# Loads, stores and zero fill of a decode layer's backward pass: one DMA queue in a fixed order instead of two side by side

## The chip, the cores and the metric

The kernel runs on one core of a Trainium2 chip. A core has a matrix engine (TensorE, PE in the profile), three engines for vectors and elements (VectorE, DVE; ScalarE, ACT; GpSimd, POOL) and SyncE (SP), which here only issues DMAs. Data move between the device memory and the on-chip memory through 16 DMA engines. A DMA is issued by an engine's instruction stream, in order: an instruction that waits for a semaphore holds up all that stand behind it in the same stream. The metric is the device time of one execution in microseconds; lower is better.

## The reference

A layer with pre-normalised sliding-window attention over a cache and a gated feed-forward part, for one decoded token in each of two batch rows, and the gradients of its eight inputs:

```python
def _A_ref(x, k_cache, v_cache, wq, wo):          # Hq 32, Hkv 8, Dh 128, Sk 32768, W 4096
    q = (x @ wq) ...
    k = jnp.repeat(k_cache[:, :, Sk - W:, :], rep, axis=1)
    v = jnp.repeat(v_cache[:, :, Sk - W:, :], rep, axis=1)
    p = _softmax(einsum("bhqd,bhkd->bhqk", q, k) * Dh ** -0.5)
    return einsum("bhqk,bhkd->bhqd", p, v) ... @ wo

def _B_ref(x, w_gate, w_up, w_down):
    return (_gelu(x @ w_gate) * (x @ w_up)) @ w_down

h = x + _A_ref(_layernorm(x), k_cache, v_cache, wq, wo)
h2 = h + _B_ref(_layernorm(h), w_gate, w_up, w_down)
# outputs: h2 and, for the given grad_out, d x, d k_cache, d v_cache, d wq, d wo, d w_gate, d w_up, d w_down
```

Only the last 4096 of 32768 cache rows take part. So the gradients of both caches (2 x 8 x 32768 x 128 in bf16 each) are zero in the other 28672 rows of every one of the 16 (batch row, group) pairs. Those zeros have to be written: 32 regions of 7 MiB, 224 MiB together.

## The kernel before, in words

**Stages.** Batch row b is handled as `attention(b)`, `middle(b)` and `score_grads(b)`, first for b = 0 and then for b = 1; after that come the weight gradients and the cache gradients.

- `attention(b)` runs over eight groups g, each with its 4096 keys K(b,g) and values V(b,g), 1 MiB each. For a group, PE transposes the keys (`kt_unit`, L378, in four units), multiplies them with the queries (`s_unit`, L388), a softmax follows (`softmax`, L392 to L415), and then eight units of products of keys and probabilities (`m_unit`): four element-wise products on DVE into one of the small `pK` buffers (L422) and the matmuls into `oPK_ps` (L429) and `M_ps` (L433). In the code the transposes and softmax of group g + 1 are woven into the units of group g. `finish` copies the group's sums out (L438 to L441).
- `middle(b)` does the output projection, the feed-forward part forwards and backwards, and the way back through `wo`. Its first matmul (L522) needs the row of x, which is loaded again for b = 1 (`load_rows`, L135).
- `score_grads(b)` transposes the values (L656) and forms the gradient of the scores. For b = 1 the weight gradients `wo`, `w_down`, `w_gate`, `w_up` are made piece by piece between its units (`grad_units`, L727) and stored when a group of pieces is whole (L737, L755, L762).
- Then follow `wq` (L807, stores at L810) and the cache gradients: 16 stores of 2 MiB (L836 for the matmuls, L844 for the stores) out of eight staging buffers.

**Memory.** Keys, values and weights share one block of on-chip memory with fixed offsets. K(0,g) has four slots of its own, so that K(0,g+4) can be loaded only after group g is finished. V(b,g) has one slot for each g; V(1,g) can be loaded only after score_grads(0) has transposed V(0,g). K(1,0), K(1,1) go to the `w_down` slot, K(1,2) to K(1,4) into the value slots 5 to 7, K(1,5) into the slot of K(1,0), K(1,6) into that of K(1,1), and K(1,7) into that of K(1,5). V(1,5) to V(1,7) follow into the slots of K(1,2) to K(1,4).

**Order.** SyncE and GpSimd issue in the order of the program text (`manual_schedule`, L676). The order of PE, DVE and ACT is made by a planner, which uses estimated costs and arrival times of the loads; it is fixed when the kernel is built. `prefetch(b, g)` (L306) is called at the start of each group and stands for the place in the text at which loads are issued. All loads but two rows go on SyncE's queue, and so do the stores of the weight gradients. GpSimd makes the zero tile `zt` (one row of 2048 bytes per partition; the DMA widens it to 32-bit zeros) after `wq` has landed (L315). It then issues 29 of the 32 regions (`zero_cast`), with nothing in between. The last three regions are cut in pieces of 1, 1, 1, 2, 2 MiB (`ZERO_CUTS`) and follow the 16 stores of the cache gradients, one piece after each but the last (`zero_next`).

In three regions a part of the zeros is written with 15 or 12 rows instead of 128 (`ZERO_PARTS`), so that not all of the DMA engines get an equal share there. In the built kernel each DMA of GpSimd waits for the completion of the one eight before it.

Of the kernel before, what the change touches and what calls it, by code (L numbers as in the profile page):

```python
# [8 lines left out]
F32 = mybir.dt.float32  # L9
U8 = mybir.dt.uint8  # L10
U32 = mybir.dt.uint32
ACT = mybir.ActivationFunctionType
ALU = mybir.AluOpType
# [3 lines left out]
P = 128  # L17
# [7 lines left out]
F = 1792  # L25
# [43 lines left out]
def kernel(ctx, tc, A_x, A_k_cache, A_v_cache, A_wq, A_wo, B_x, B_w_gate, B_w_up, B_w_down, grad_out,  # L69
# [36 lines left out]

    ZERO_PARTS = {8: ((4, 1), (15, 2), (2, 2), (15, 14), (12, 2), (P, 4), (16, 7)), 16: ((4, 1), (15, 2), (2, 2), (15, 14), (12, 2), (P, 4), (16, 7)), 24: ((3, 16), (15, 2), (3, 4), (15, 18), (12, 2), (P, 4))}
    ZERO_FIRST, ZERO_CUTS = 29, (1, 1, 1, 2, 2)

    def zero_cast(i):  # L110
        dst, done = zero_regions[i].bitcast(F32), 0
        for rows, n in ZERO_PARTS.get(i, ((P, ZPK // P),)):
            src = zt[0:rows * (P // rows):P // rows, :]
            nc.gpsimd.dma_start(out=dst[done * ZE:(done + rows * n) * ZE].rearrange("(p k e) -> p k e", p=rows, k=n),  # L114
                                in_=src.unsqueeze(1).to_broadcast([rows, n, ZE]))
            done += rows * n
        assert done == ZPK

    zero_pieces = []
    for i in range(ZERO_FIRST, len(zero_regions)):  # L120
        done = 0
        for k in ZERO_CUTS:
            zero_pieces.append(zero_regions[i].bitcast(F32)[done:done + P * k * ZE].rearrange("(p k e) -> p k e", p=P, k=k))
            done += P * k * ZE
        assert done == ZPK * ZE

    def zero_next():
        if zero_pieces:
            dst = zero_pieces.pop(0)
            nc.gpsimd.dma_start(out=dst, in_=zt[:].unsqueeze(1).to_broadcast([P, dst.shape[1], ZE]))  # L130

# [16 lines left out]

    def load_k(b, g):
        Kt[b, g] = at(K_OFF[b][g], [P, NJ, DH], BF16, f"K{b}_{g}")  # L150
        nc.sync.dma_start(out=Kt[b, g][:], in_=Kv[:, b, g, :, :])

    def load_v(b, g):
        Vt[b, g] = at(OFF_V + g * 8 * KIB, [P, NJ, DH], BF16, f"V{b}_{g}")
        nc.sync.dma_start(out=Vt[b, g][:], in_=Vv[:, b, g, :, :])

# [10 lines left out]
    def load_wg():  # L167
        nc.sync.dma_start(out=wg[:], in_=B_w_gate.rearrange("(p r) f -> p r f", r=NDR))

    def load_wu():  # L170
        nc.sync.dma_start(out=wu[:], in_=B_w_up.rearrange("(p r) f -> p r f", r=NDR))

# [133 lines left out]
    def prefetch(b, g):  # L306
        if b == 0:
            if g == 0:
                load_k(0, 0)
                load_wd(OFF_WD0)  # L310
                load_v(0, 0)
                for i in range(1, 4):
                    load_k(0, i)
                    load_v(0, i)
                nc.gpsimd.tensor_scalar(out=zt[:], in0=wq_sb[:, 0, 0:ZE // 2].bitcast(U8),  # L315
                                        scalar1=0, scalar2=None, op0=ALU.mult)
                for i in range(ZERO_FIRST):
                    zero_cast(i)
            elif g + 3 < HKV:
                load_k(0, g + 3)  # L320
                load_v(0, g + 3)
            elif g == 5:
                nc.sync.dma_start(out=wo_sb[:], in_=A_wo.rearrange("(p r) n -> p r n", r=NOR))
            elif g == 6:
                load_wg()
            elif g == HKV:
                load_wu()
                load_k(1, 0)
                load_k(1, 1)
        else:  # L330
            if g == 0:
                for i in range(5):
                    load_v(1, i)
                for i in range(2, 5):
                    load_k(1, i)
            elif g == 1:
                load_k(1, 5)
            elif g == 2:
                load_k(1, 6)
            elif g < 6:  # L340
                load_v(1, g + 2)
            elif g == 6:
                load_k(1, 7)
            elif g == HKV:
                load_rows(nc.sync)
                load_wd(OFF_WD)
# [351 lines left out]
    with tc.tile_pool(name="ps_G", bufs=2, space=PSUM) as ps_G:  # L698
# [35 lines left out]

        for (r0, nr) in ((0, 14), (14, 14), (28, 4)):
            add_group([D] * nr, lambda k, r0=r0: Ro_flat[:, (r0 + k)::NOR], lambda k: DH_bf[:],
                      lambda st, r0=r0, nr=nr: nc.sync.dma_start(out=gwo_v[:, r0:r0 + nr, :],  # L737
                                                                 in_=st[:, :nr * D].rearrange("p (a n) -> p a n", n=D)))
        row_box = {}

        def rows_from_T(key, srcT_bf):
# [3 lines left out]
            for r in range(NFR):  # L745
                if r == 8:
# [7 lines left out]
        add_group([D] * NFR, lambda k: row_box["act"][:, k::NFR], lambda k: dh2_bf,  # L754
                  lambda st: nc.sync.dma_start(out=gwd_v, in_=st[:, :NFR * D].rearrange("p (a n) -> p a n", n=D)))  # L755
        for (key, srcT, o_dram) in (("dg", dgT_bf, out_6), ("du", duT_bf, out_7)):
            grad_units.append(lambda key=key, srcT=srcT: rows_from_T(key, srcT))
            o_v = o_dram.rearrange("(p r) f -> p r f", r=NDR)
            pieces = [(r, f0, fl) for r in range(NDR) for (f0, fl) in ((0, 512), (512, 512), (1024, 512), (1536, 256))]
            add_group([fl for (_, _, fl) in pieces], lambda k, pieces=pieces: ln2_bf[:, pieces[k][0]::NDR],  # L760
                      lambda k, key=key, pieces=pieces: row_box[key][:, pieces[k][1]:pieces[k][1] + pieces[k][2]],
                      lambda st, o_v=o_v: nc.sync.dma_start(out=o_v, in_=st[:, :NDR * F].rearrange("p (r f) -> p r f", r=NDR)))  # L762
        g_next = [0]
# [9 lines left out]
    with tc.tile_pool(name="ps_W2", bufs=2, space=PSUM) as ps_W, \  # L773
# [27 lines left out]
        for r in range(NDR):  # L801
            st = at(OFF_WQ + r * 8 * KIB, [P, HQ * DH], BF16, "gq")
            for c4 in range(4):
                ps = ps_G.tile([P, 1024], F32, tag="ps_g", name="ps_gq")
                for q in range(2):
                    col0 = c4 * 1024 + q * 512
                    nc.tensor.matmul(out=ps[:, q * 512:(q + 1) * 512], lhsT=L_bf[:, r::NDR],  # L807
                                     rhs=Ro_flat[:, col0:col0 + 512], start=True, stop=True)
                evac(st[:, c4 * 1024:(c4 + 1) * 1024], ps[:])
            nc.sync.dma_start(out=gwq_v[:, r, :], in_=st[:])  # L810

    with tc.tile_pool(name="ps_G3", bufs=3, space=PSUM) as ps_G, \
# [4 lines left out]
        def bd_of(n):  # L817
# [3 lines left out]
            return build_bd(OFF_BD + n * 8 * KIB, rowsb[:], f"bd{n}")  # L821
        nxt = bd_of(0)
        for n, (b, what) in enumerate(jobs):
            rhs_bd = nxt
            lhs_bf, dst_v = (ds_bf[b], dKv) if what else (p_bf[b], dVv)
            for gq in range(2):
# [15 lines left out]
                for a in range(2):  # L842
                    g0 = gq * 4 + a * 2
                    nc.gpsimd.dma_start(out=dst_v[:, b, g0:g0 + 2, :, :], in_=sts[a][:])  # L844
                    zero_next()
                if gq == 0 and n + 1 < len(jobs):
# [28 lines left out]
```

## Time and profile before

| What | Value |
| --- | --- |
| Median of 3 runs | 791.56 us (791.41 to 791.93) |
| Profiled execution, own time | 791.69 us |
| Its span, first to last instruction | 790.0 us |
| Mean granted TensorE clock | 0.807 |
| PE, DVE, ACT, POOL busy | 72%, 60%, 36%, 8% |
| Bytes moved by DMA | 332.44 MB, mean 421 GB/s |
| HBM read, written | 49.30 MB, 282.33 MB |
| attention(0), last matmul of `M_ps` | ends at about 135 us |
| attention(1), matmuls of `M_ps` | about 250 to 387 us |
| First store of a weight gradient issued (L737) | 484.2 us |
| First store of a cache gradient issued (L844) | 619.8 us |

The page cuts the span into 40 equal slices of 19.75 us. Its DMA row gives the mean busy share of the 16 DMA engines in tenths, its GB/s row what they moved. The queue rows give packets, megabytes, and the time that the packets took as a share of 16 engines' span: q0 is GpSimd's queue, q1 SyncE's; packets of two queues overlap in time, so that the shares may sum to more than one. In the rows of waits the numbers are the time in total, how often, and the longest. In a timeline each row has the start, the duration, the engine and the line, and in brackets how long the engine had been idle before and what ended that.

### The profile page before, as it was taken

Reading aid. Unit: us, or ns where it says so; the run is one execution under the profiler, and the core shown is the slowest. Engines: PE = TensorE matmul, PEld = TensorE weight load, DVE = VectorE, ACT = ScalarE, POOL = GpSimd, SP = SyncE. Lnnn points to the kernel's source line nnn. Section 1 sums busy time; section 2 is a strip of 40 time slices with the busy share of each in tenths; the row PEclk is TensorE's granted clock in tenths of the full one; section 3 lists DMA queues with packets and bytes.
Section 4 is the critical chain, followed back from the end, with each engine's and each line's share of the span. In section 5 each row is a group of like instructions: output and inputs, shape, how many; then the busy total and the mean of one; then the engine's idle time right before and its main releaser. Section 6 shows DMA issues by size and latency. Waiting matters only on the chain. (4 is left out here: it accounts for less than half of the span.)

```text
span 790.0 us, 12468 instructions
## 1 busy us (share of the span) xinstructions
PE 564.9 (72%) x5096; PEld 301.0 (38%) x5096; DVE 472.6 (60%) x1161; ACT 280.9 (36%) x406; POOL 65.5 (8%) x97
## 2 busy tenths in 40 slices
PE   3899998795888899825558779797886775857000
PEld 3655554544665555313225544343332221212000
DVE  2699998238335899824612676755457998757000
ACT  1534330234344433102012426544443674646000
POOL 4300000000020000000020000000100111111100
PEclk9899999786799999877876869855685897779555
DMA  8999999999999999999999999999999999999997
GB/s 366 416 419 422 419 424 428 424 430 427 428 419 418 426 424 426 425 425 430 427 428 428 428 428 427 422 430 424 430 426 427 424 430 426 428 428 427 428 429 295
DMA packets 41418, 332.44 MB, mean 421 GB/s; under 512 B 2432, under 2 KB 2448, under 8 KB 2576
## 3 DMA queue, kind: packets, MB, share of 16 engines
q0 software_dynamic: 34416, 268.44, 88.6%
q1 hardware_dynamic: 6932, 63.19, 37.5%
q8 instruction: 40, 0.66, 0.3%
q10 hardware_dynamic: 12, 0.01, 0.2%
q14 instruction: 18, 0.15, 0.0%
HBM read 49.30 MB, written 282.33 MB: 420 GB/s over the span
## 5 line engine op out<-in xcount | busy, mean ns | idle before, releaser
L422 DVE TENSOR_TENSOR mem<-mem,ee 128x512 bf16<-128x512 bf16 x512 | 180.6, 414 | 34.0 <-PE M_ps L433 33.8
L433 PE MATMUL M_ps<-mem 128*128 128x512 bf16 x512 | 140.2, 392 | 5.3 <-DVE mem L422 4.8
L836 PE MATMUL ps_g<-mem 128*128 128x512 bf16 x256 | 85.6, 448 | 38.4 <-DVE mem L91 36.8
L91 DVE CAST mem<-ps_g 128x512 bf16<-128x512 f32 x128 | 82.9, 686 | 26.7 <-DMA out_dram<-mem 15.3
L93 ACT CAST mem<-ps_g 128x512 bf16<-128x512 f32 x128 | 74.3, 586 | 51.4 <-PE ps_g L836 49.5
L380 ACT COPY mem<-KT_ps 128x1024 bf16<-128x1024 bf16 x64 | 63.1, 1013 | 77.4 <-PE KT_ps L378 72.7
L114 POOL DMA_DIRECT2D out_dram<-zt x46 | 36.9, 976 | 503.6 <-DMA out_dram<-zt 503.2
L378 PE MATMUL KT_ps<-ident_bf,mem 128*128 128x128 bf16 x512 | 44.7, 229 | 28.3 <-DMA mem<-in_A_k_cache_dram 23.3
L836 PEld LDWEIGHTS <-mem 128*128 128x128 bf16 x256 | 28.1, 110 | 95.3 <-issue 84.7
L433 PEld LDWEIGHTS <-mem 128*128 128x128 bf16 x512 | 43.8, 99 | 48.8 <-issue 15.5
L254 PE MATMUL ps_tb<-ident_bf,mem 128*128 128x128 bf16 x480 | 55.9, 250 | 7.1 <-ACT mem L258 2.7
L93 ACT COPY mem<-ps_tb 128x512 bf16<-128x512 bf16 x44 | 25.8, 586 | 67.5 <-PE ps_tb L254 62.7
L254 PEld LDWEIGHTS <-mem 128*128 128x128 bf16 x480 | 37.4, 128 | 32.3 <-issue 31.0
L656 PE MATMUL VT_ps<-ident_bf,mem 128*128 128x128 bf16 x512 | 46.8, 239 | 2.6 <-ACT mem L93 1.1
L665 PE MATMUL dP_ps<-mem 128*128 128x512 bf16 x128 | 44.3, 435 | 4.5 <-ACT mem L93 4.5
L656 PEld LDWEIGHTS <-mem 128*128 128x128 bf16 x512 | 36.6, 107 | 27.9 <-issue 20.5
L378 PEld LDWEIGHTS <-mem 128*128 128x128 bf16 x512 | 33.7, 103 | 34.0 <-DMA mem<-in_A_k_cache_dram 23.9
L93 ACT COPY mem<-VT_ps 128x1024 bf16<-128x1024 bf16 x31 | 31.7, 1022 | 34.0 <-PE VT_ps L656 32.8
L91 DVE COPY mem<-ps_tb 128x512 bf16<-128x512 bf16 x44 | 18.7, 424 | 41.6 <-PE ps_tb L254 40.2
L727 PE MATMUL ps_gr<-mem 2*128 2x512 bf16 (+1 forms) x78 | 33.7, 498 | 11.7 <-DVE mem L747 7.4
L91 DVE CAST mem<-ps_gr 128x512 bf16<-128x512 f32 (+1 forms) x38 | 24.7, 654 | 27.9 <-PE ps_gr L727 27.9
L91 DVE COPY mem<-VT_ps 128x1024 bf16<-128x1024 bf16 x33 | 23.1, 700 | 28.0 <-PE VT_ps L656 27.5
(244 smaller groups left out, 619.7 us busy)
## 6 DMA issues: line engine op xcount, KB each, us to landing
out_dram<-zt POOLq DMA_DIRECT2D x26, 7168.0 KB, 102.4
out_dram<-mem POOLq DMA_DIRECT2D x16, 2048.0 KB, 34.0
mem<-in_A_k_cache_dram SPq DMA_DIRECT2D x16, 1024.0 KB, 20.7
mem<-in_A_v_cache_dram SPq DMA_DIRECT2D x16, 1024.0 KB, 21.4
out_dram<-zt POOLq DMA_DIRECT2D x3, 4096.0 KB, 58.5
out_dram<-zt POOLq DMA_DIRECT2D x6, 2048.0 KB, 33.0
out_dram<-zt POOLq DMA_DIRECT2D x9, 1024.0 KB, 34.6
out_dram<-mem SPq DMA_DIRECT2D x5, 1792.0 KB, 18.7
```

The lines of the kernel that those rows point to most:

```text
L91: nc.vector.tensor_copy(out=out, in_=in_)
L93: nc.scalar.copy(out=out, in_=in_)
L114: nc.gpsimd.dma_start(out=dst[done * ZE:(done + rows * n) * ZE].rearrange("(p k e) -> p k e", p=rows, k=n), in_=src.unsqueeze(1).to_broadc ...
L254: nc.tensor.transpose(out=ps[:, a, :], in_=src_block(a), identity=ident_bf[:])
L378: nc.tensor.transpose(out=KT_ps[:, jj, :], in_=Kt[b, g][:, u * 8 + jj, :], identity=ident_bf[:])
L380: nc.scalar.copy(out=KT[:], in_=KT_ps[:])
L422: nc.vector.tensor_tensor(out=pk[:, :, i, :].rearrange("p j (d t) -> p j d t", t=2), in0=Kb[:, j0:j0 + pk_j, :].rearrange("p j (d t) -> p ...
L433: nc.tensor.matmul(out=M_ps[:], lhsT=Vt[b, g][:, j, :], rhs=pk[:, jj, :, :].rearrange("p i d -> p (i d)"), start=(j == 0), stop=(j == NJ - 1))
L656: nc.tensor.transpose(out=VT_ps[:, jj, :], in_=Vt[b, g][:, a * 8 + jj, :], identity=ident_bf[:])
L665: nc.tensor.matmul(out=dP_ps[:, c, :], lhsT=dOpad[:, w0:w0 + P], rhs=VT[:, c * 4:(c + 1) * 4, :].rearrange("d a k -> d (a k)"), start=(i = ...
L727: nc.tensor.matmul(out=ps[:, :n], lhsT=lhsT_fn(k), rhs=rhs_fn(k), start=True, stop=True)
L836: nc.tensor.matmul(out=ps[:, a2, :], lhsT=lhs_bf[:, jp * P:(jp + 1) * P], rhs=rhs_bd[:, ap * 2 + a2, gq * 4:(gq + 1) * 4, :].rearrange("q ...
```

## The change

Key, value, `wo`, `w_gate` and `w_up` loads and the stores of the weight gradients move from SyncE's to GpSimd's queue. The zeros are counted in columns of 1 MiB (224 in all), and `zeros(n)` issues the next n of them. Each load or store on GpSimd's queue is followed by a fixed number of columns. What stays on SyncE: x, `wq`, K(0,0), V(0,0), K(0,1), V(0,1), `w_down` both times, K(1,7), the rows for the second half, and the gradient of x. The zero tile is now made from K(0,0) instead of `wq`, and the first zeros follow K(0,2) to V(0,3). The three regions with unequal parts are 5, 15 and 26 instead of 8, 16 and 24, with somewhat different parts.

```diff
-    ZERO_PARTS = {8: ((4, 1), (15, 2), (2, 2), (15, 14), (12, 2), (P, 4), (16, 7)), 16: (...same...), 24: ((3, 16), (15, 2), (3, 4), (15, 18), (12, 2), (P, 4))}
-    ZERO_FIRST, ZERO_CUTS = 29, (1, 1, 1, 2, 2)
+    ZERO_PARTS = {5: ((4, 1), (15, 2), (2, 2), (15, 18), (12, 1), (128, 4), (16, 4)), 15: (...same...), 26: ((3, 16), (15, 2), (3, 4), (15, 18), (12, 2), (128, 4))}
+    TAIL_ZEROS = (1, 1, 1, 2, 2, 1, 1, 1, 2, 2, 1, 1, 1, 2, 2, 0)
+    def zeros(n):
+        while n:
+            i, c = divmod(z_cols[0], ZCOLS)
+            parts = ZERO_PARTS[i] if c == 0 and n >= ZCOLS and i in ZERO_PARTS else ((P, min(n, ZCOLS - c)),)
+            done = c * P
+            for rows, k in parts:
+                zero_rows(zero_regions[i].bitcast(F32)[done * ZE:(done + rows * k) * ZE], rows, k)
+                done += rows * k
+            z_cols[0] += done // P - c
+            n -= done // P - c
...
-        nc.sync.dma_start(out=Kt[b, g][:], in_=Kv[:, b, g, :, :])
+        eng.dma_start(out=Kt[b, g][:], in_=Kv[:, b, g, :, :])       # eng=nc.gpsimd unless given; V alike
...
     def prefetch(b, g):
             if g == 0:
-                load_k(0, 0)
+                load_k(0, 0, nc.sync)
                 load_wd(OFF_WD0)
-                load_v(0, 0)
-                for i in range(1, 4):
+                for i in range(2):
+                    load_v(0, i, nc.sync)
+                    if i == 0:
+                        load_k(0, 1, nc.sync)
+                nc.gpsimd.tensor_scalar(out=zt[:], in0=Kt[0, 0]...)
+                for i in range(2, 4):
                     load_k(0, i)
                     load_v(0, i)
-                nc.gpsimd.tensor_scalar(out=zt[:], in0=wq_sb...)
-                for i in range(ZERO_FIRST):
-                    zero_cast(i)
+                zeros(5)
             elif g + 3 < HKV:
                 load_k(0, g + 3)
+                zeros(1)
                 load_v(0, g + 3)
+                zeros(2)
             elif g == 5:
-                nc.sync.dma_start(out=wo_sb[:], ...)
+                nc.gpsimd.dma_start(out=wo_sb[:], ...)
+                zeros(2)
             elif g == 6:
                 load_wg()
+                zeros(7)
             elif g == HKV:
                 load_wu()
                 load_k(1, 0)
                 load_k(1, 1)
+                zeros(29)
         else:
             if g == 0:
                 for i in range(5):
                     load_v(1, i)
+                    zeros(1)
                 for i in range(2, 5):
                     load_k(1, i)
+                    zeros(1 if i < 4 else 8)
             elif g == 1:
                 load_k(1, 5)
+                zeros(5)
             elif g == 2:
                 load_k(1, 6)
+                zeros(5)
             elif g < 6:
                 load_v(1, g + 2)
+                zeros((5, 6, 60)[g - 3])
             elif g == 6:
-                load_k(1, 7)
+                load_k(1, 7, nc.sync)
...
+        def store(out, in_, n):
+            nc.gpsimd.dma_start(out=out, in_=in_)
+            zeros(n)
-        for (r0, nr) in ((0, 14), (14, 14), (28, 4)):        # wo gradient, stores on nc.sync
+        for (r0, nr, nz) in ((0, 14, 3), (14, 14, 1), (28, 4, 9)):   # stores by store(..., nz)
...                                                          # w_down: store(..., 8); w_gate 5; w_up 13
-            nc.sync.dma_start(out=gwq_v[:, r, :], in_=st[:])
+            nc.gpsimd.dma_start(out=gwq_v[:, r, :], in_=st[:])
+            zeros(1 if r < NDR - 1 else 10)
...
                     nc.gpsimd.dma_start(out=dst_v[:, b, g0:g0 + 2, :, :], in_=sts[a][:])
-                    zero_next()
+                    zeros(tail_zeros.pop(0))
```

## The prediction

> **What bounds the kernel now.** First the 40 slices of the page, then its DMA queues and the chain of waits:
>
> ```profile
> DMA  8999999999999999999999999999999999999997
> GB/s 366 416 419 422 419 424 428 424 430 427 428 419 418 426 424 426 425 425 430 427 428 428 428 428 427 422 430 424 430 426 427 424 430 426 428 428 427 428 429 295
> q0 software_dynamic: 34416, 268.44, 88.6%
> q1 hardware_dynamic: 6932, 63.19, 37.5%
> ```
>
> The DMA engines are busy from the second slice to the last. 332.4 MB must move, 268.4 of them on GpSimd's queue (q0), 63.2 on SyncE's (q1). No compute engine is near its limit (PE 72%, DVE 60%), so the kernel ends when the bytes are through: the chain's largest item is the stores at the end (14% of the span). A change can help only by a higher rate and hurt only by time in which no transfer is queued. The rate is not the same everywhere. Windows (us, engines, then clock, DMA share, GB/s):
>
> ```profile
> 20.00:60.00 40.00, 37.55 (x529) 24.68 (x527) 32.14 (x101) 17.98 (x23) 7.56 (x9) 0.91 1.13 417
> 160.00:200.00 40.00, 30.24 (x276) 19.64 (x275) 23.63 (x62) 16.29 (x30) 1.29 (x2) 0.76 1.15 429
> 210.00:250.00 40.00, 32.72 (x423) 22.87 (x422) 13.99 (x29) 20.97 (x22) 5.77 (x6) 1.00 1.14 421
> 420.00:480.00 60.00, 46.85 (x382) 27.07 (x381) 37.56 (x97) 23.41 (x41) 1.71 (x3) 0.77 1.15 427
> ```
>
> Where only zeros move (160:200, 420:480) it is 427 to 429; where SyncE's loads mix in (20:60, 210:250), 417 to 421. Then what GpSimd waits for:
>
> ```profile
> POOL out_dram L114 <- DMA out_dram<-zt: 503.2, 30, 37.2
> 19.35 7.61 POOL L114 DMA_DIRECT2D out_dram<-zt  x8 [0.31 <-POOL zt L315]
> 59.10 0.60 POOL L114 DMA_DIRECT2D out_dram<-zt  x1 [32.14 <-DMA out_dram<-zt]
> 619.82 0.73 POOL L844 DMA_DIRECT2D out_dram<-mem  x1 [60.29 <-DVE mem L91]
> ```
>
> Eight DMAs go out, and each further one waits for the one eight before it. A zero region is 7 MiB, so up to 56 MiB lie ahead: GpSimd's 60.3 us wait before the first cache-gradient store leaves the DMA engines busy all the same. SyncE's DMAs are those that wait on compute:
>
> ```profile
> 206.42 17.68 SPq L155 DMA_DIRECT2D mem<-in_A_v_cache_dram  x5
> 291.63 30.78 SPq L155 DMA_DIRECT2D mem<-in_A_v_cache_dram  x3
> 335.20 0.33 SPq L151 DMA_DIRECT2D mem<-in_A_k_cache_dram  x1
> 484.19 14.30 SPq L737 DMA_DIRECT2D out_dram<-mem  x3
> ```
>
> These are a V load for each slot that score_grads(0) frees, three V loads paced by groups 2 to 4 of the second attention, K(1,7) after group 5, and the wo gradient. Today a late one costs no DMA time, because zeros fill in. Last, how long K(1,7) takes to arrive (PE in time):
>
> ```profile
> 339.73 0.81 PE L433 MATMUL M_ps<-mem 128*128 128x512 bf16 x3
> 363.26 1.89 PE L378 MATMUL KT_ps<-ident_bf,mem 128*128 128x128 bf16 x16 [22.72 <-DMA mem<-in_A_k_cache_dram]
> ```
>
> Issued at 335.20, used at 363.26: 28 us behind the zeros for 1 MiB.
>
> **What the skill says.** "DMA: Bandwidth & Descriptors", "Issuing engines are not separate DMA queues": all issuers run on the same 16 engines, and another issuer saves sequencer time only. The trace agrees on the shared engines (417 to 430 in all mixtures), yet mixing costs up to 2.5%. The same page, "SWDGE vs HWDGE vs iDMA", says that an engine round-robins between the queues; 28 us for a 2.45 us transfer fits. Its "Latency and other measured facts" puts a GpSimd DMA's first byte at about 1 us; here the zeros issued at 19.35 show in the byte counts only after 23 us, with SyncE's loads ahead. "SBUF — State Buffer", "SBUF: two separate sides", warns that GpSimd cannot write descriptors while VectorE holds the shared port; nothing here tests it, since GpSimd is always far ahead.
>
> **The change part by part.**
>
> *Rate.* Summing the shortfall from 428 over slices 2 to 38 gives 90 slice-GB/s; 90 / 428 x 19.75 us = 4.15 us. Of q1's 63 MB about 13 stay on SyncE (first loads, K(1,7), w_down), mostly with nothing beside them; I leave 0.45 us for those. Gain 3.7 us. Bounds: 0, if reads rather than two queues cost the rate; about 6, if loads alone run above 428.
>
> *The bytes.* Same 224 columns of 1 MiB of zeros, same loads and stores; the tail keeps 1,1,1,2,2 three times. The rows that skip one DMA engine (16, 16, 20 to 20, 20, 20) and the 69 more DMAs on GpSimd (146 for 77; 0.5 to 0.95 us each, engine 8% busy) cost nothing while transfers are queued.
>
> *The queue in order.* Now a waiting load or store stops all zeros behind it, and the DMA engines live on what was queued. I put 1 MiB at 2.45 us (428 GB/s) and start from 366 GB/s x 19.75 us = 6.9 MiB done at 19.75. SyncE's first 9.75 MiB, four loads and 5 zeros last to 48.8. Each later share ends at: prefetch 1 to 4 (5 MiB each) 61.0, 73.3, 85.5, 97.8; wo 112.5; gate 133.9; up with 29 zeros 214.2; five V 238.7; three K 270.5; K(1,5) 285.2; K(1,6) 299.9; V(1,5) 314.6; V(1,6) 331.8; V(1,7) with 60 zeros 481.2, and with K(1,7) and w_down (2.75 MiB on SyncE) 488.0. When today's compute releases the next item: 44.1, 57.7, 71.1, 84.1 (K(0,4) to K(0,7)), 106.1 gate, 128.6 up, 206.4 V(1,0), 262.2 K(1,5), 278.1, 291.6, 305.2, 322.1, 484.2 the wo gradient. The queue outlasts each, by 1.4 us (K(0,7)) to 9.7; at the wo gradient by 3.8. After it the reserves are 4 to 8 us, at the cache stores 25. With today's compute times nothing drains.
>
> *But the compute order changes.* Built, the two kernels differ on PE, DVE and ACT: the planner sees later loads and moves work of the second attention. From the start of that attention, with today's durations (a group's 32 products 32 x 0.345 = 11.0, a softmax in their gaps 2.4, oPK copy 0.4; keys transposed and softmax with nothing beside, 240.08 to 248.28 = 8.2):
> - Groups 0 and 1: softmax 1 waits less than it did, group 1 ends near 274 on DVE, 274.5 on PE.
> - Group 2's key transposes now stand behind group 1's last matmul: 274.5 + 8.2 = 282.7, and 1.5 because its first matmuls stand behind group 3's transposes. Its end: 298 (now 291.5). V(1,5) then goes out 2 us before the queue is dry at 299.9.
> - Group 3 with softmax 4: 311.5; group 4: 322.9. Group 5's transposes begin late in group 4, its scores end at 325.3, softmax to 328.5, 8 products to 331.2; then softmax 6 in one piece to 335.3, 24 products to 343.7.
> - K(1,7) is issued at 343.7 instead of 335.2: +8.5. It stays on SyncE; taking 26.4 us (29, 22 and 28 us for the last three loads of this attention): -1.6.
> - On PE its transposes now stand ahead of all of group 6's matmuls, where now 11 are already done: +4.0 after it lands.
>
> Sum +10.9 us at the end of the attention. The x row (12.7 us on SyncE) and middle(1) keep their times and follow on the path, so the wo gradient is ready at 484.2 + 10.9 = 495.1. Queued behind it on GpSimd are its 3 zeros and all later stores; the queue is dry at 488.0: 7.1 us idle, and 2 for the restart (from 1, the page's first byte, to 4.4, the first zeros here): 9.1. Later waits come less late than the queue has by then been shifted, so they add nothing.
>
> Sum on the profiled execution: 790.0 - 3.7 + 9.1 = 795.4 span, 1.7 around it (791.69 against 790.0; the median is 791.56, 0.1 lower): **797.0 us**.
>
> **Rivals.**
> 1. *Nothing drains* (faster). It decides if the wo gradient is ready by about 486, an attention at most 2 us later. For it: the shares fit today's release times well; K(1,7) could land in 20 us. Against: the order. 790.0 - 3.7 + 1.7 = 788.0.
> 2. *The rate does not rise*, because reads, not a second queue, cost it ("does not do what it says"). The page cannot part these. With no drain 791.6; with the drain the last bytes come about as in the forecast, since the late store sets them.
> 3. *GpSimd is starved or drains at several places*: four waits of the first attention have 1.4 to 4.7 us reserve, less than a 4.4 us restart, and descriptors must be written while DVE runs products. 5 us at each of two or three more places, or two PE gaps like those of 2.5 and 3.3 us in today's second attention: 803 to 812.
>
> **Numbers.** Forecast, a drain of 5 to 15 us: 0.52 (792.5 to 802, own range). Rival 1: 0.22. Rival 2 or a drain that only eats the gain: 0.12. Rival 3: 0.14. Within 0.2% (1.6 us, about what this measurement can tell) lie rival 2 and the forecast's edge. Faster 0.22, same 0.13, slower 0.65. Low end 787.5 for rival 1; high end 805 leaves out the worse half of rival 3.
>
> **What would show it.** Right: q1 down to about 13 MB; 427 to 430 GB/s in slices 2 to 17; one notch in the DMA row near 488 to 497 us, with GpSimd waiting there on the wo gradient's copies; PE idle before key transposes near 345 to 370. Rival 1: no notch. Rival 2: 418 to 422 in slices 2 to 5 with the queue full. Rival 3: notches near 50 to 100 us. The forecast falls if K(1,7) is issued before 338, or if the second attention ends before 391.

## The result, and the profile after

The changed kernel takes 808.97 us (median of four executions, 808.52 to 813.06) against 791.66 us before (791.41 to 791.93): a ratio of 1.0232, 95% interval [1.0203, 1.0261]. The profiled execution is the longest of the four, 813.06 us with a span of 811.3; sums over the trace are made against that one.

The page of the changed kernel, its slices of DMA and its two queues:

```profile
DMA  8999999999999999999999994799999999999996
GB/s 368 410 423 412 421 424 427 430 425 429 425 426 428 427 412 394 427 427 428 429 432 425 429 427 165 292 427 431 427 430 426 425 432 427 427 428 427 427 429 266
q0 software_dynamic: 40640, 318.52, 102.5%
q1 hardware_dynamic: 1172, 13.12, 5.7%
```

One notch in two slices (165 and 292 GB/s) where the kernel before had 427 and 422. Slices 15 and 16 are lower too (412 and 394 for 424 and 426), and slices 2 and 4 (410 and 412 for 416 and 422); the others flow about as fast as before or faster. The same stretch in windows of 10 us (us, busy time of the engines, then clock, DMA share, GB/s):

```profile
480.00:490.00 10.00, 6.37 (x62) 4.38 (x59) 8.64 (x25) 4.13 (x9) 0.00 (x0) 0.50 1.13 422
490.00:500.00 10.00, 8.69 (x73) 4.63 (x72) 7.05 (x12) 1.25 (x2) 0.00 (x0) 0.66 0.55 203
500.00:510.00 10.00, 9.48 (x67) 4.46 (x66) 6.68 (x13) 6.25 (x9) 0.00 (x0) 1.00 0.00 2
510.00:520.00 10.00, 10.00 (x76) 4.75 (x74) 6.78 (x10) 6.48 (x10) 1.31 (x2) 1.00 0.69 274
```

Against 428 GB/s these four windows lack 6 + 225 + 426 + 154 GB/s; divided by 428 and times 10 us that is 18.9 us without data. In the middle two, GpSimd issues nothing (x0) while TensorE and VectorE work. What it waits for, first from its waits (total, times, longest), then from its timeline (start, duration, idle time before and what ended it):

```profile
POOL out_dram L745 <- DVE mem L91: 123.7, 1, 123.7
POOL out_dram L114 <- DMA out_dram<-zt: 102.3, 22, 19.2
```

```profile
386.96 1.64 POOL L114 DMA_DIRECT2D out_dram<-zt  x2 [2.90 <-DMA out_dram<-zt]
512.34 0.55 POOL L745 DMA_DIRECT2D out_dram<-mem  x1 [123.73 <-DVE mem L91]
512.88 0.77 POOL L114 DMA_DIRECT2D out_dram<-zt  x1
```

From 388.6 us on GpSimd stands at the first wo-gradient store (L745). What it had queued by then lasts to 494.7 us on the mean of the engines (513.6, where the data flow again, less 18.9); the zeros queued behind the store go out only with it, at 512.88. Why the store is late is in the second attention, on TensorE and on SyncE's queue:

```profile
349.66 1.02 PE L442 MATMUL M_ps<-mem 128*128 128x512 bf16 x4 [0.32 <-DVE mem L431]
379.97 1.89 PE L387 MATMUL KT_ps<-ident_bf,mem 128*128 128x128 bf16 x16 [28.95 <-DMA mem<-in_A_k_cache_dram]
384.51 1.89 PE L442 MATMUL M_ps<-mem 128*128 128x512 bf16 x4
```

```profile
349.67 0.33 SPq L148 DMA_DIRECT2D mem<-in_A_k_cache_dram  x1
412.59 0.25 SPq L133 DMA_DIRECT2D mem<-in_grad_out_dram  x1
```

Group 5 ends at 350.7, and TensorE then idles 28.95 us for K(1,7), one of the few loads left on SyncE. Only after its transposes (L387) come group 6's products (384.51): two groups wait for one load. The attention ends at 412.6 (SyncE's x and gradient rows go out at 412.59), 25.2 us later than before.

### The profile page after: what moved, and what is told of

It is laid out like the page before. It is cut to its first block, busy times and chain, and to the rows that moved or that the text cites. A ratio compares the mean times of both kernels' runs of the same rounds, so it can differ in the third digit from the quotient of the medians.

```text
span 811.3 us, 12540 instructions
## 1 busy us (share of the span) xinstructions
PE 576.3 (71%) x5096; PEld 302.5 (37%) x5096; DVE 475.0 (59%) x1161; ACT 280.6 (35%) x406; POOL 101.3 (12%) x166
## 5 line engine op out<-in xcount | busy, mean ns | idle before, releaser
L851 PE MATMUL ps_g<-mem 128*128 128x512 bf16 x256 | 81.1, 414 | 33.1 <-DVE mem L91 28.6
L91 DVE CAST mem<-ps_g 128x512 bf16<-128x512 f32 x128 | 82.0, 687 | 18.8 <-DMA out_dram<-mem 10.8
L114 POOL DMA_DIRECT2D out_dram<-zt x90 | 60.8, 746 | 120.1 <-DMA out_dram<-zt 102.3
L387 PE MATMUL KT_ps<-ident_bf,mem 128*128 128x128 bf16 x512 | 45.5, 236 | 30.6 <-DMA mem<-in_A_k_cache_dram 28.9
L387 PEld LDWEIGHTS <-mem 128*128 128x128 bf16 x512 | 34.9, 106 | 38.0 <-DMA mem<-in_A_k_cache_dram 29.0
L736 PE MATMUL ps_gr<-mem 2*128 2x512 bf16 (+1 forms) x78 | 33.7, 496 | 11.8 <-DVE mem L760 7.4
```

Of the source, the lines that this page charges most:

```text
L91: nc.vector.tensor_copy(out=out, in_=in_)
L114: nc.gpsimd.dma_start(out=dst.rearrange("(p k e) -> p k e", p=rows, k=n), in_=src.unsqueeze(1).to_broadcast([rows, n, ZE]))
L387: nc.tensor.transpose(out=KT_ps[:, jj, :], in_=Kt[b, g][:, u * 8 + jj, :], identity=ident_bf[:])
L736: nc.tensor.matmul(out=ps[:, :n], lhsT=lhsT_fn(k), rhs=rhs_fn(k), start=True, stop=True)
L851: nc.tensor.matmul(out=ps[:, a2, :], lhsT=lhs_bf[:, jp * P:(jp + 1) * P], rhs=rhs_bd[:, ap * 2 + a2, gq * 4:(gq + 1) * 4, :].rearrange("q ...
```

## The experiments

Each kernel was compared with the kernel before in the same set of runs (791.6 to 792.0 us).

### First set: four ways to remove the notch

*70 columns of zeros ahead of the first store instead of 60* (the ten are taken from later shares):

```diff
-                zeros((5, 6, 60)[g - 3])
+                zeros((5, 6, 70)[g - 3])
```

> Ten more columns of zeros stand ahead of the first wo-gradient store (70 instead of 60), ten fewer later (w_up 9 instead of 13, last wq store 4 instead of 10; the region with unequal parts is 27 instead of 26). The orders of PE and DVE are those of the changed kernel. Theory 'the queue runs dry in front of a store that waits': the wo store is still ready at about 512 us, but the queue lasts to about 518, so the notch of some 19 us goes and the time falls from 809 to 789-793. Rival 'late compute': the lateness of the second attention (25 us) is what sets the end, with or without a notch; the time stays at 803-810. Rival 'GpSimd cannot keep the queue supplied': the rate between notches is below 425 GB/s and the time stays above 800.

Measured: 800.36 us, ratio 1.0109 [1.0094, 1.0124].

*The weight-gradient stores back on SyncE* (those of wq by the same edit at their own line), shares unchanged:

```diff
-            nc.gpsimd.dma_start(out=out, in_=in_)
+            nc.sync.dma_start(out=out, in_=in_)
```

> One part undone: the stores of the weight gradients go on SyncE again, the zeros that followed them stay in the same order on GpSimd. The late second attention stays. Theory 'the queue runs dry in front of a store that waits': GpSimd passes on to 48 more columns, no notch before the wo store (the 2 us one near 304 stays), 789-794. Rival 'late compute': 803-810. Rival 'not supplied': above 800.

Measured: 800.07 us, 1.0105 [1.0088, 1.0122].

*The loads back on SyncE*, the stores stay on GpSimd:

```diff
-    def load_k(b, g, eng=nc.gpsimd):
+    def load_k(b, g, eng=nc.sync):
```

(the same for V, wo, gate and up)

> The other part undone: all loads go on SyncE again, the stores of the weight gradients stay on GpSimd with their shares of zeros. The orders of PE and DVE in the second attention are then those of the kernel before. Theory: the second attention ends near 388 again, the wo store is ready at 484-488, the zeros last to about 490, so no notch; the rate beside the loads falls back to 417-421; 788-793. Rival 'a store in GpSimd's stream costs by itself': a notch stays before the wo store although it is early, 800 or more.

Measured: 800.03 us, 1.0105 [1.0090, 1.0120].

*K(1,7) on GpSimd's queue, ahead of most of the large share*:

```diff
-                zeros((5, 6, 60)[g - 3])
+                zeros((5, 6, 6)[g - 3])
             elif g == 6:
-                load_k(1, 7, nc.sync)
+                load_k(1, 7)
+                zeros(54)
```

> K(1,7) goes on GpSimd's queue after 6 of the 60 columns, with 54 behind it, instead of on SyncE's. It is ready to be issued near 350 and then stands behind what is queued to about 357, so it lands near 360 instead of 380. The planner puts its transposes behind group 6, whose matmuls no longer wait. Theory 'K(1,7) behind the zeros and the order built on it make the second attention late': it ends near 385-390 instead of 412.6, the wo store is ready at 484-490, little or no notch, 788-793. Rival 'the lateness comes from the order of groups 2 to 5': it ends no earlier than 400, a notch of 8 us or more stays, 797-805.

Measured: 800.65 us, 1.0114 [1.0099, 1.0129].

The notch of 165 and 292 GB/s is gone in all four. The data rows (GB/s in 40 slices) of the kernel with the loads back on SyncE and of the one with K(1,7) on GpSimd:

```profile
GB/s 368 421 419 421 419 425 427 423 426 428 427 419 421 424 424 426 425 426 427 429 427 429 427 427 428 426 432 427 431 424 426 429 430 426 428 428 427 428 428 115
```

```profile
GB/s 369 409 423 396 413 430 428 426 426 429 426 426 427 427 428 408 425 424 426 430 427 429 427 426 428 427 430 431 430 424 426 430 429 427 429 428 426 429 430 119
```

Two things follow. The notch is made by the pair of a late store and the zeros behind it: with 70 columns the store still goes out at 511.5 us, and with the stores on SyncE at 511.5 too, both without that notch, since the zeros do not run out or do not stand behind it. With the loads on SyncE, or with K(1,7) alone on GpSimd, the store itself is back at 484.3, where it was before (484.19). GpSimd's timeline with 70 columns, and then with the loads on SyncE:

```profile
511.52 0.55 POOL L745 DMA_DIRECT2D out_dram<-mem  x1 [113.24 <-DVE mem L91]
```

```profile
484.26 0.55 POOL L745 DMA_DIRECT2D out_dram<-mem  x1 [95.39 <-DVE mem L91]
```

But all four end at 800, and had been expected at 788 to 794: their last slice holds 115 and 119 GB/s in the two rows shown, where the kernel before had 295. A second cause is left, of 8.3 to 8.9 us if it is the same in all four.

### Second set: the row counts of the uneven zero regions

In three regions the zeros are cut into parts of fewer than 16 rows, so that not all 16 DMA engines get a packet of 8 KiB. The change has other counts in two of them. Four kernels vary these alone, two made from the kernel before and two from the one with 70 columns. *The new counts in the kernel before*:

```diff
-(15, 14), (12, 2), (P, 4), (16, 7)      # regions 8 and 16
+(15, 18), (12, 1), (128, 4), (16, 4)
```

> The kernel before with the changed kernel's row counts in its two unequal zero regions (8 and 16): (15,18), (12,1), (128,4), (16,4) for (15,14), (12,2), (128,4), (16,7); nothing else. A part of 15 rows leaves one of the 16 DMA engines out of every packet, so the new counts take about 4 packets of 8 KiB more off one engine in each of the two regions; at 427 GB/s over 16 engines such a packet is 0.31 us. Theory A (the common remainder of 8.4 us in the four variants comes from the new row counts: the engines no longer end together): 798 to 800 us. Rival B (the row counts are not it; another engine load, of smaller zero DMAs or of the GpSimd queue itself, makes one engine late): 791 to 793 us.

Measured: 798.60 us, 1.0089 [1.0074, 1.0104].

*The old counts in the kernel with 70 columns* (the reverse edit, regions 5 and 15):

> The changed kernel with 70 columns of zeros ahead of the first wo-gradient store, and the kernel before's row counts (15,14), (12,2), (128,4), (16,7) in regions 5 and 15. Theory A (row counts): the last data comes at 787 to 789 us instead of 795.4, and the time is 788 to 792 us. Rival B (not the row counts): the late engine loses 8 packets of relief, 2.5 us, and the time is 800 to 803 us.

Measured: 797.25 us, 1.0073 [1.0058, 1.0088].

*No uneven parts at all*, `ZERO_PARTS = {}`, in the kernel before and in the one with 70 columns:

> The kernel before with all zero regions as equal rows (no unequal parts at all): shows how late the latest engine comes by itself. By the old counts one engine is spared about 12 packets in each of two regions and 14 in the third, 38 x 0.31 = 11.8 us in all. If that engine was the one that ends last and the sparing just levels it: about 802 to 804 us under both theories. If the sparing does nothing: 791.5.

Measured: 803.49 us, 1.0149 [1.0134, 1.0165].

> The changed kernel with 70 columns ahead of the first wo-gradient store, all zero regions as equal rows. The new counts spare one engine about 16 + 16 + 14 = 46 packets, 14.3 us. Theory A (the engine is spared too much or the wrong one, and others end late for it): 796 to 803 us, about as before_equal or below it. Rival B (the late engine is later here by itself, and the sparing only falls short): 800 + 14 = 812 to 816 us, some 10 us above before_equal.

Measured: 804.87 us, 1.0164 [1.0147, 1.0181].

The end of the kernel before without uneven parts, in windows (last columns: DMA share, GB/s), and then one window of the kernel before as it is:

```profile
780.00:786.00 6.00, 0.00 (x0) 0.00 (x0) 0.00 (x0) 0.00 (x0) 0.00 (x0) 0.50 0.58 236
786.00:792.00 6.00, 0.00 (x0) 0.00 (x0) 0.00 (x0) 0.00 (x0) 0.00 (x0) 0.50 0.06 26
792.00:800.00 8.00, 0.00 (x0) 0.00 (x0) 0.00 (x0) 0.00 (x0) 0.00 (x0) 0.50 0.06 24
```

```profile
786.00:792.00 6.00, 0.00 (x0) 0.00 (x0) 0.00 (x0) 0.00 (x0) 0.00 (x0) 0.50 0.02 8
```

A share of 0.06 is 1 of 16, and 26 GB/s is 427/16: from 786 us on a single DMA engine works, and it ends at 799.1, 13 us after the other 15. One engine falls behind the rest, and the uneven parts are what keeps it from setting the end: with them the kernel before ends 11.9 us earlier. The new counts spare it too little, 4.9 us of the 11.9, though by the count of rows they should spare it more. In the kernel with 70 columns they bring about as little, 4.5 us (804.87 to 800.36); its 804.87 lies between the two expected ranges, nearer to that of theory A.

That engine is not slower at all times. In the packet records of the same trace each zero region ends with 16 packets of 4 bytes; read as one for each engine, they tell when an engine was through with its share. For the engine that comes last, the share from 366 to 383 us took 17.3 us, the same as the middle one of the others, and 142 instructions began in that time. Five of its shares between 383 and 512 us, with 239 to 363 instructions in each, took 17.6 to 18.0 us, and the middle one of the others 17.0 to 17.1. After 786 us, when no instruction runs, its packets of 8 KiB follow each other every 0.306 us, which is 1/16 of 427 GB/s. So it loses time while the other engines of the core work; that the work is the reason was not tested.

The kernel with 70 columns and old counts is a partial miss: its engines do end within 2 us of each other (790.2 to 792.0), but the ten columns were taken from later shares, and a notch of 334 GB/s stands in its slice 34 (360 with the new counts, in the kernel with 70 columns of the first set). So it can't give the price of the row counts by itself.

### Third set: the order of the counts, and the two causes apart

*The new counts in one region only*: first (region 8), or last (region 24, with the set of 24 in 8). The three sets of counts are the same in both:

```diff
+    ZERO_PARTS = {8: NEW, 16: OLD, 24: OLD_24}     # first
+    ZERO_PARTS = {8: OLD_24, 16: OLD, 24: NEW}     # last
```

> The kernel before with the new row counts, (15,18), (12,1), (128,4), (16,4), in region 8 alone; regions 16 and 24 as in the kernel before. With the new counts in both regions the time was 798.6 us: one engine ended 3.8 us earlier than with no unequal rows at all (795.3 for 799.1), which is about 12 packets of 0.31 us, one region's worth of sparing. Theory S (the part (12,1) goes to another number of engines than (12,2), so the order in which the engines are taken does not come back, and every later unequal part spares another engine): only the first region spares the right engine, and the time is again 797 to 799.5 us. Rival L (each region with the new counts spares less by itself, wherever it stands): half of the loss, 794 to 796 us.

Measured: 802.50 us, 1.0136 [1.0121, 1.0151].

> The same three sets of row counts as in the kernel with the new counts first, in another order: the set of the kernel before's region 24 in region 8, its set of region 16 in region 16, and the new counts in region 24, with no unequal part after them. Theory S (order of the engines shifted by (12,1)): nothing follows that could be shifted, so all three regions spare the same engine and the time is 790.5 to 793.5 us. Rival L (the new counts spare less by themselves): 794 to 796 us, as with the new counts first.

Measured: 790.58 us, 0.9984 [0.9977, 0.9991].

Windows of the end, of the kernel with the new counts first and then of the one with them last:

```profile
786.00:792.00 6.00, 0.00 (x0) 0.00 (x0) 0.00 (x0) 0.00 (x0) 0.00 (x0) 0.50 0.14 56
792.00:800.00 8.00, 0.00 (x0) 0.00 (x0) 0.00 (x0) 0.00 (x0) 0.00 (x0) 0.50 0.05 20
```

```profile
786.00:792.00 6.00, 0.00 (x0) 0.00 (x0) 0.00 (x0) 0.00 (x0) 0.00 (x0) 0.59 0.01 5
792.00:800.00 8.00, 0.00 (x0) 0.00 (x0) 0.00 (x0) 0.00 (x0) 0.00 (x0) 1.00 0.00 0
```

The same sets of row counts in another order move the time by 11.9 us. Rival L, which gives both the same time, is refuted. The likeliest reading is that the order decides which engine a part leaves out. The Trainium skill, "DMA: Bandwidth & Descriptors", "Why a DMA increments its semaphore by 16 and not by 1", says that a GpSimd DMA with k < 16 shares goes to k consecutive engines from a round-robin cursor; that fits, and no view here names an engine. By such a count, against 56 packets per engine in an even region, the left-out engine gets 45 with the old set, 41 with the new one, 40 with region 24's set, where three others get 68 to 70. If all three regions spare the slow engine, it saves 11 + 11 + 16 = 38 packets of 0.31 us, 11.8 us, in the kernel before (measured 799.1 to 787.9: 11.2), and 16 + 11 + 15 = 42 with the new counts last (its last data at 786.9). With the new counts first, sparing 15 packets there and then hitting the 12 to 14 extra packets in region 24 gives 1 to 3, 0.3 to 0.9 us; measured 799.1 to 798.3, 0.8 us. I had expected 797 to 799.5 us for that kernel, because I had left out the three overloaded engines. On this account the new set shifts the cursor for all that follows. Its rows sum to 48 like the old set's; the part that differs in kind is (12,1). That (12,1) is the one that shifts is argued, not shown.

*The changed kernel with the old counts*, and *the kernel with K(1,7) on GpSimd with the old counts*:

> The changed kernel with the kernel before's row counts in regions 5 and 15, shares of zeros and queues unchanged. If the changed counts and the queue that runs dry add up: the engines end together, but all of them have lost the dry stretch, 485 to 515 us, and the time is 800 to 805 us, 4 to 9 us below the changed kernel. If the dry stretch alone made the changed kernel's 17 us: 808 to 810.

Measured: 812.29 us (809.25 to 812.97), 1.0253 [1.0234, 1.0273]: the row counts alone give nothing back. The range for two causes that add, 800 to 805, is missed.

> The changed kernel with K(1,7) on GpSimd's queue ahead of 54 of the 60 columns, and the kernel before's row counts in regions 5 and 15: both suspected causes undone, all else of the change in place. With the new counts it took 800.65 us. If the two causes are all: the engines end together at 786 to 788.5 us of the span, and the time is 789.5 to 793 us, the kernel before's within 0.25%. If a third cause is left (the cutting of the zeros into shares, the queue of the stores): 795 to 800.

Measured: 793.68 us, 1.0025 [1.0016, 1.0034]: with both causes undone the kernel is back within 2 us, just outside the expected 789.5 to 793.

### Fourth set: what makes K(1,7) late, and what is left

*The second attention in the written order of instructions*, `tc.manual_schedule(...)` around `attention(1)`; the transfers keep their queues and order:

> The changed kernel with the instructions of the second attention in the order in which they are written, instead of the planner's; SyncE's and GpSimd's queues issue the same transfers in the same order. In the changed kernel K(1,7) is used at 380.0 us and only then TensorE starts on group 6 (384.5 us), though group 5 ended at 350.7; the attention ends at 412.6. Theory O (the order makes group 6 wait for K(1,7) too): group 6 runs before 380, the attention ends at 395 to 402 us, the first wo-gradient store is issued 10 to 17 us earlier, at 495 to 502, the dry stretch shrinks to 3 to 10 us and the time is 798 to 805 us. Rival W (the wait for K(1,7) alone makes the lateness): the attention ends at 408 to 413 us, the time stays at 808 to 813.

Measured: 821.13 us, 1.0362 [1.0343, 1.0381]. A miss that decides nothing: in this order the groups themselves run slower, K(1,7) goes out only at 366.2 us and is used at 392.5, and group 6 still stands behind it (393.8 to 413.8). From K(1,7)'s first use to the end of the attention it takes 32.6 us, as in the changed kernel.

*K(1,7) on GpSimd and two edits for the small dry stretches*, three columns more in the first share and three behind K(1,6), with region 24's set first and the new counts last (the lines of the row counts are not shown):

```diff
-                zeros(5)
+                zeros(8)
...
-                zeros(29)
+                zeros(26)
...
                 load_k(1, 6)
-                zeros(5)
+                zeros(8)
...
                 load_k(1, 7)
-                zeros(54)
+                zeros(51)
```

> The changed kernel with K(1,7) on GpSimd's queue ahead of the large share, as before, and three more edits: three columns of zeros more in the first share (8 for 5, from the 29), three more behind K(1,6) (8 for 5, from the 54), so that the queue is not empty at 60 to 104 and 302 to 309 us; and the order of row counts that gave 790.6 in the kernel before: region 24's set in region 5, the set of 16 in region 15, the new counts in region 26. Working: k17_old_parts took 793.68 us; its small dry stretches are 2.2 us at 302 and some 1.5 us at 60 to 104; the level order of row counts gave 1.2 us in the kernel before. Together 793.7 - 3.7 - 1.2 = 788.8; expected 787.5 to 791 us, the first below the kernel before. If something else in the change takes the gain of the data rate: 792 to 795.

Measured: 796.09 us, 1.0050 [1.0035, 1.0065]. A miss: the three columns at the start stand ahead of the next loads of the first attention, which runs late from its second group on (group 7 ends at 146.3 us instead of 136.3 in the changed kernel), and the queue runs short at 150 and 270 us instead (364 and 372 GB/s in 10 us).

*K(1,7) on SyncE, all else as in the kernel of 793.68 us*, one word:

```diff
-                load_k(1, 7)
+                load_k(1, 7, nc.sync)
                 zeros(54)
```

> The variant with K(1,7) ahead of the large share and the kernel before's row counts (793.68 us), with one word changed: K(1,7) is on SyncE's queue instead of GpSimd's, still with 6 of the 60 columns ahead of it and 54 behind it in the program. Theory Q (the queue makes it late: on SyncE it shares the engines with all that GpSimd's queue holds, before it and behind it): K(1,7), issued at about 350 us, is used 26 to 30 us later instead of 11.5, at 376 to 380, TensorE's order waits for it with group 6, the first wo-gradient store comes at 505 to 513 instead of 482, the queue runs dry and the time is 803 to 813 us. Rival D (the columns ahead of it make it late): it is used by 366 us, the store comes before 490 and the time is 793 to 796 us.

Measured: 811.05 us, 1.0248 [1.0234, 1.0262]. The whole loss comes back with it. Without the word (K(1,7) on GpSimd), timelines of GpSimd and TensorE:

```profile
350.25 0.55 POOL L148 DMA_DIRECT2D mem<-in_A_k_cache_dram  x1 [19.37 <-PE M_ps L443]
482.23 0.55 POOL L746 DMA_DIRECT2D out_dram<-mem  x1 [94.03 <-DVE mem L91]
```

```profile
360.79 1.02 PE L443 MATMUL M_ps<-mem 128*128 128x512 bf16 x4 [0.32 <-DVE mem L432]
362.02 1.05 PE L388 MATMUL KT_ps<-ident_bf,mem 128*128 128x128 bf16 x16
```

With the word (K(1,7) on SyncE), timelines of SyncE, TensorE and GpSimd, and the row of data:

```profile
351.61 0.34 SPq L148 DMA_DIRECT2D mem<-in_A_k_cache_dram  x1
```

```profile
380.49 1.89 PE L388 MATMUL KT_ps<-ident_bf,mem 128*128 128x128 bf16 x16 [27.53 <-DMA mem<-in_A_k_cache_dram]
385.03 1.89 PE L443 MATMUL M_ps<-mem 128*128 128x512 bf16 x4
```

```profile
510.77 0.55 POOL L746 DMA_DIRECT2D out_dram<-mem  x1 [124.11 <-DVE mem L91]
```

```profile
GB/s 369 409 424 406 420 421 427 430 426 427 427 426 427 428 421 382 427 428 428 427 431 428 428 427 209 293 428 429 430 428 427 426 431 427 427 429 426 428 428 284
```

On GpSimd K(1,7) is used 11.8 us after its issue (362.02 - 350.25), on SyncE 28.9 us (380.49 - 351.61). The attention ends at 413.3 instead of 383.9, 29.4 us later: 1.4 from the issue, 17.1 from the longer flight, and 10.9 from group 6's products, which ran before K(1,7)'s transposes on the one side (360.79 belongs to group 6) and behind them on the other (385.03). The planner made that change of order with the edit; the two were not parted. In the program 54 columns stand behind the load. With the word, GpSimd's stream has no load to wait for and goes on to the zeros from 332 us on, before SyncE issues the load at 351.61, so the one word also lets the zeros pass the load.

The packet records of the traces divide the flight on SyncE. In the changed kernel K(1,7) is issued at 349.67 us. Its first packet of data moves at 360.25 and its last ends at 366.21. With it go 16 packets of 4 bytes, which start as the data end, at 365.2 to 366.5 us, and end only at 376.4 to 379.5; TensorE starts 0.5 us after the last of them, at 379.97. So of 30.3 us the 1 MiB itself took 6.0, after a wait of 10.6, and then came 13.2 us in which the data had been moved and only these packets were open. The kernel with the one word has the same three parts (10.8, 5.8 and 11.9 us), and so has the kernel before (6.7, 7.1 and 13.7). On GpSimd's queue in the changed kernel no packet of 4 bytes takes more than 0.09 us. What holds these packets on SyncE's queue was not followed.

*K(1,7) on GpSimd, three more columns behind K(1,6), and the level order of the row counts*:

> The variant with K(1,7) on GpSimd's queue ahead of the large share (793.68 us with the kernel before's row counts), with three more columns behind K(1,6), 8 for 5 from the 54, and the order of the row counts that gave 790.58 us in the kernel before. The dry stretch at 302 us cost 2.15 us of data flow there. If it and the level of the engines are what is missing: 790.3 to 791.8 us, the kernel before's time within 0.2%. If the extra columns ahead of V(1,5) cost the attention as much again, as in the variant with six extra columns: 793.5 to 796 us.

Measured: 792.22 us, 1.0005 [0.9997, 1.0014]: level with the kernel before, not below it. Its rates:

```profile
GB/s 367 411 423 403 418 431 427 426 426 428 427 425 426 426 428 427 427 427 426 426 430 429 428 426 420 424 430 429 430 427 428 427 431 427 428 427 428 428 429 272
```

The shortfall from 428 over slices 2 to 38 is 81, 3.7 us, against 4.1 for the kernel before. Without the first four of these slices it is 1.1 against 2.5 us: the higher rate is there, 1.4 us. But slices 2 to 5 (411, 423, 403, 418) lack 57 where the kernel before lacked 36, which takes 1.0 us of it back.

The two causes in the changed kernel, as the four runs give them:

| | K(1,7) on GpSimd, no notch | K(1,7) on SyncE, notch |
|---|---|---|
| old row counts | 793.68 | 811.05 |
| new row counts | 800.65 | 808.97 (the change itself) |

(The second column differs also in where the program has the share of zeros, ahead of K(1,7) or behind it; the changed kernel with old counts, 812.29, says that this is small.) They do not add: 17.4 us for the notch alone, 7.0 for the counts alone, 15.3 for both. The engine that lags has more left when the others run dry. In the changed kernel the last zeros ahead of the store landed at 501.4 us, 6.7 us after the mean of the engines had run dry, so that engine lost 12 us in the notch where the mean lost 18.9.

## Why the prediction was wrong, point by point

I predicted 797.0 us (787.5 to 805), slower by one dry stretch of GpSimd's queue. Direction, place and cause were right, the size was not: the dry stretch took 18.9 us and not 9.1, because the second attention ended 25.2 us late and not 10.9. A smaller part of the miss, 4.9 us, is the forecast gain of 3.7 us in the rate, in whose place all else cost 1.2.

- **The queue runs dry in front of the wo-gradient store** (step "the queue is dry at 488.0: 7.1 us idle, and 2 for the restart"). One notch at that place came, and no other of its size. The term was mis-sized: 18.9 us instead of 9.1. The queue was dry at 494.7 (6.7 later than worked out), the store was issued at 512.34 instead of 495.1 (17.2 later), the restart took 1.3 instead of 2. 17.2 - 6.7 - 0.7 is the difference of 9.8.
- **When the store is ready** (step "the compute order changes", sum +10.9). It became +25.2 at the end of the attention. K(1,7) was issued at 349.67 instead of 343.7: +6.0 on the forecast. It flew 30.3 us instead of 26.4: +3.9. From its use to the end it took 32.6 us instead of 28.2: +4.4. So all three terms of the last load were short, each in the same direction. Another 2.9 us came between the attention and the store, where I had said that the stages "keep their times"; in the timelines it is spread over them, 0.3 to 1.0 us in each of five parts, and why was not followed. The one-word experiment shows how much hangs on this load: 17.4 us of time. I had also said that the 28 us of K(1,7) in the kernel before fit an engine that takes turns between two queues. By the packet records only the 7.1 us in which its data move are of that kind; the 6.7 us before them and the 13.7 behind them are not explained by it.
- **The rate** ("Gain 3.7 us"). Partly right. The windows at 210:250, 421 GB/s before, gave 426, but 20:60 went from 417 to 416. The kernel without notch shows a gain of 1.4 us after the first five slices and a loss of 1.0 in them. The step took the whole shortfall for the cost of two queues; what the first slices lack is not of that kind.
- **The row counts** ("cost nothing while transfers are queued"). This step failed, and the range had no place for it: in the kernel before the new counts cost 7.0 us, and in the kernel with K(1,7) on GpSimd, without the notch, also 7.0. The engines do not end together by themselves; one of them ends 13 us late unless it is spared. So a change can also hurt while transfers are queued, which "hurt only by time in which no transfer is queued" left out. In the changed kernel this cost is covered by the notch, so it is not what made the forecast miss.
- **Only one place drains.** V(1,5), issued at 302.65 against a queue that I had dry at 299.9, did cost a small stretch: 338 GB/s from 300 to 310, 2.1 us.

The sum, on the span: the forecast was 795.4, the measurement 811.3, 15.9 more. Of these 9.8 are the notch. The last data came 20.1 us later than before (808.06 for 787.94), so all else than the notch made +1.2 us instead of the -3.7 of the rate: 4.9. The remaining 1.2 us are the end of the program after the last data, 3.2 us for 2.0.

Rival 1 (nothing drains) and rival 2 (the rate alone) fell with the notch. Rival 3 had the right size with the wrong mechanism, since the extra loss is not spread over several places. My condition "the forecast falls if the second attention ends before 391" did not come up; a late end, at 412.6, was not weighed.

A version that beats both kernels is the kernel before with only the order of its row counts changed (new counts last): 790.58 us, 0.16% below the kernel before.

## What to carry to other kernels

When a queue that carries work for the DMA engines is also made to wait for compute, its reserve must be set against the worst lateness of that compute, and the lateness must be followed through the one load that the last group waits for, on whatever queue it flies. A load of 1 MiB that is alone on a second queue beside a full first one is not a fast load: K(1,7) took 22 to 31 us on SyncE's queue in the kernels here, and 10.4 to 16.1 us on GpSimd's, with few zeros ahead of it. Before counting a change of transfer shapes as nothing, look at how many engines still work in the last slices: a DMA share of 0.06 is one of sixteen.

## What the runs showed of the hardware that was not expected

- With all zeros cut evenly, one of the 16 DMA engines ends 13 us after the others (786 to 799.1 us at 24 to 26 GB/s). It does not lag evenly: its share of a zero region took it 17.6 to 18.0 us for 17.0 to 17.1 with 239 to 363 instructions beside it, and 17.3, as for the others, with 142.
- A load on SyncE's queue beside GpSimd's full one had moved its 1 MiB 16.5 us after its issue, but its closing packets of 4 bytes ended only 13.2 us later (K(1,7) in the changed kernel).
- A change in the order of three sets of uneven row counts, the same bytes and DMAs, moved the time by 11.9 us (790.58 to 802.50).
- The late end of one engine and a dry stretch of all of them overlap almost wholly: 17.4 and 7.0 us apart, 15.3 together.
